# A two-image residual block: one statistics buffer shifted by 64 elements, two memsets dropped, one vector group moved behind another

## The chip, the cores and the metric

The kernel runs on one core of a Trainium2 chip. Its time is the device time of one execution in microseconds (us). Five engines work side by side, each through its own instructions in a fixed order, and wait for one another through semaphores: TensorE (PE in the profile: matmuls; PEld: its weight loads), VectorE (DVE), ScalarE (ACT), GpSimd (POOL) and SyncE (SP), which here only issues DMA transfers.

## The reference

Two images of 512 channels and 64x64 pixels go through a residual block of a diffusion network:

```
h   = conv3(silu(group_norm(x, g1, be1)), w1)        # 4 groups, 3x3 filters, zero padding
h   = h + (silu(t_emb) @ w_emb)[:, :, None, None]
out = x + conv3(silu(group_norm(h, g2, be2)), w2)
```

A group norm needs the mean and the variance of 128 channels x 4096 pixels before its first SiLU can start. Everything is bf16 at the edges.

## The kernel before

**Tiling.** The 512 channels are four tiles (`ct` 0 to 3) of 128 partitions. An image is worked in two chunks of 32 rows, so that there are eight chunks: first layer image 0 (chunks 0 and 1) and image 1 (2 and 3), then the second layer likewise. Nearly all data lies in one SBUF array, `ar`, at offsets that are worked out by hand; `Z` is a scratch region in it.

**Convolution.** It is a fast convolution in the row direction. From the rows of an input tile the vector engine makes transformed planes; TensorE multiplies each with transformed filters; results are combined again. For chunk 0 and tile `ct` the steps on DVE are eight instructions on a scratch buffer `WB[ct % 3]`:

- `k0ct`: one scaling of 2210 elements a partition (`rows_a`, line 678; issued by `ts`, L349);
- `row0ct`: three adds of 1040 elements (`rows_a`; `tt`, L345). The third gives planes 4 and 5;
- `rob0ct`: an add, a scaling of 520 elements, and two adds (`rows_b`, line 692). These give planes 0 to 3.

Tile 1's scratch is `WB[1]`, at `Z` to `Z + 2210`; tile 2's begins at `Z + 6528`.

**Opening.** ACT applies the SiLU to tile 0 and tile 1 (`silu00`, `silu01`), each followed by a small POOL memset of the padding column (`z00`, `z01`), for which `k00` and `k01` wait. The statistics of tiles 2 and 3 (`st02`, `st03`, in `stats0`, line 1131) go around the engines: ones- and Gram-matmuls on PE, an ACT Square over 2080 elements, a small DVE product with the identity (L1190), an ACT Identity over 260 elements of PSUM, a tiny fp32 matmul on PE, then small DVE and POOL steps (L466 to L491), and the SiLU of the tile. PE then runs 24 groups of three matmuls called `o` (planes 4 and 5 with three sets of filters, tile 0 first), and after that `u00` (planes 0 to 3, tile after tile). PE fills its wait ahead of them with dummy matmuls on `ones_bf`. Meanwhile DVE also transforms the filters (`w1_0`, `w1_1`: adds of 1536 elements).

**The second image's statistics.** `stats1` (line 1225) loads each tile of image 1 in two halves into `ZST` and `ZST + 2080`, and ACT reads each half twice (2080 elements, L368). The first of these loads is called `st10`; in the SP queue it stands behind five loads of filter pieces (`ld_ur..`) and ahead of more of them, of `a10` (the input of chunk 1, into `AB[0]`), of `w1_1` and of the following statistics loads.

**Order.** No scheduler runs. Each operation is recorded in a plan with a number, and `ORDER` (line 168), a string with two characters for each operation, gives the order in which all of them are issued; an engine takes its own from it. Waits are set by overlap of the memory that operations read and write: an operation waits for earlier ones in that order that touch the same elements.

Of the kernel before, what the change touches and what calls it, by code (L numbers as in the profile page):

```python
# [165 lines left out]


ORDER = (
    "0P0M000N2i0R0Q0O0n010S020304050607080m0T1I0l1F0c0k1G0i0r0d0j1H0o0q0p0e0s1K1J1L0t0u0f0v1M0w1N0V1O2b1P0x0y260W0z0-2Y0g0h1Q"
# [3 lines left out]
    "483F3j5g3H493k4m3G4A4g3Y5Y4o4B4n4C3X3l4D4f3I4E4p4F3J3_3M4q4I3s403K4J3L6d3m4K3o4r4L3r4M5a4i4y4_4N3N4O5b5h5i4P3u3O55454s41"
    "56424v4R575Z4t584h3v59515A4G6V524Q5B4H5C4w4-6r5F5j5G4u6e6f5H5l436s5I445J5c6t5K5m5L8C5M6X5n5k5u50465p4z5v8D5w4S6W5x8E5z5o"
    "5-4T4W535_BU4UBV60543P4V615d4X6263475r4Y5q645N6Y9H5O675E6g685D5s69BW5P3Q6A5t6C6i6D5Q5T5e6E6h5R6j6F5SBY6G6B6kBk9I6H5y7-6l"
    "6a6I5U6J6u4Z6m5V6Z6v6n6w939J6x6qBX6p6z666-6_BcBZBm7071Ba657273AM746K79Bl6oBd6L7A6bBb5f6cAN4a7BAO5W7CBR7E6M7F7D7G7H6N6Q7I"
    "7J7KBoBe7L7P6OBSBg6P7QDT6y6R7RDbBn7iBfBq7S6S757j76Bp7T7kBTDc7M7UBr7l785X7mBi7VBh7W7nBj7o7p8F7q7N7r7s8G7tDU7X7u778H7v7Y7w"
    "7ODe8I7xDd7y7Z8KDV8L8M7zDf7_808N8ODX8PF18QDh8RDj8W7a8XDg7b818Y7cDQ7d8Z838S8b828a8c8d8e9495848f8g8hDRA88i858m7e8n8T878o6T"
    "7f8J868pDl8U8q8k888u8rDSDW968s8jDZ8t979K8vDY989LA9AADkDa899M999N8VBD9P8A6U9Q9R9S9T9A9U8l9VDi9W9b8B7h8w9cF29B9dDn9e9CF99g"
    "8x9h9i9j9F8z9k9l9m8y9n9G9r8-9D9sF38_9O9t9X9uDmF5909YAB9vFHF49a7g9wBEBFDp9xDoAC9yADAP9pFA9EAQ9fAE9oAR9ZDC9zAFAS9q9-AUAHAV"  # L180
    "ATAW91AX9_AYAZAGAaA3AbAgA0AcAdAhAIA2AiF7FBBGAjA1F6AlFCAmBIF8DDDEAnAoAKApAqArAsAwA4FIAxDqAJAtA5AyBJAuAzBH92A-BKEmALA_AeBM"
    "B0B2BLB1AfBsB3BNA6BtFJAvDFBuBQB4BvBPBxByB8BzB5B-AkB_C0DHB7C1C2C6DGB6C7C8C4C9B9C3CEBwCFCADIBAC5CGFLCBA7CHE-GjBOCJCKCnFDCL"
    "CMCoE_CNGbCODJFKCPCqF0CQCICTCrDLCUCVCRCWFFCZCXFECaCSDKFGBCCbFNCsDMCcGKFMDrCCGlDsDNGdGkFOCdDtCpCDEnEoCtDPDuGcDODwDxDyDzCY"
    "D-D_E2E0E1GfEpE5CuCeE6E7CvGYE8EDGnE3CwCfEEI6GeCxGrGZEFChCyEqGmEGCiCgCzErEIGLGMEJEKC-GaELEMC_EsENEOEPCjESHuETEUEAEVE9EYGh"
    "E4CkD0EZDvEtBBGpEQEaGgEHEuEbGsI8EvFPGtD1GoERFQGiD2EWEwFRECGNFSD3EBGqFUD4EzFVFWGvFXFYEcEXFZIEFaFbFdFfHvHwIAFgFhFiEdIMFnEx"
    "I7FoD5GPGuFpEeFkFqEyEgFsEhFtEfFuGQFvFeFwFxFTGwFyFzEiFcG0G1IGG2G3I9G6GRFjEjD6GxG7F-GOIFFrG8GyFlF_G9IIG4ClGSGzCmD7ICG-D8IB"
    "G_GTH0IOFmINIUGAGVH2H3JXH4IHGXH5H6GUHBH7HAH8H9G5HxHDJYJZHEIDHFHGIJHLGBEkHMIKHIHCHNGCHHDAHOHzIVGEILGFHQGWHRHSElHTHUD9H-HV"
    "HWHXGDHaH_HbGGHcHdIPHgHPHyGHHhH1HKKqKrHiIWKpI0HeHjDBI1IXIcHZHJHkIdI2NrHYIeI5JaJbI4IfNqIhHfIiIjIkIlIYImInHlIoIsIrItIQIuHp"
    "IvHmI-IqIRIpI_HoHnIaJ0IxISIwJ1IgIZITI3J3JcJ4HqJ5J6GIJ7J8J9JAIyHrJDJCJEJeJFIbJ2JGJJIzJBJfJKJHJdJLJgJIKsKtJMJiJuJnJhJvJwJj"
    "JNJlJxKuJzJ-J_JOK0K1K2JPGJK3K4K8KwK9M5KAKBJkKGKvJRKHKxPTJQKIJSJmKJM6M7K5NONPPUJTKyKLKMK6KNK7KONNK-KPKQJyKRKzKSKDKVKWKKJo"  # L190
    "KXKYKCL2KbKTK_KcKUL1KZKdM8M9KeL0LAL3JpLBKEKfLCJUMALDKFJqLFLGLHKaLILJLELKLLMCLMLOLQNQNRJrLRHsLSLTKgLYMDLZMBMELaKhKkLbPBLN"
    "JsLdKjNmNlLeMGLfKiLgLhMFQiLiLPLjJtLkHtLnLoPCPDMHNoLpLqLtMJLuPRLULVKlLvNSQhLwMKMSLXMTLcNULlMUNTLmMVNVLxMXLWQPMYLrMZL4MaNW"
    "MbMcLsMdJWMeJVMiMjL5MkMlLyMqMINpMgMrMhLzMsM0KmL-MtNXMfKnMvL_MwL6MxMyMWMzNYM-MnM_QQQRMLMmN0M1N3KoN4N5N6N9NbNAMuMpNBN1NZNC"
    "N2MoNsN7NcNtNDPSL7PEPFNuN8NdNvOmNaNxNyNENzN-PGN_M2O0O1O2OnL8O4NFO5NIOpPHO6NGPIRuNHNkO7L9M4O9OANJQfOBOCODOEOFPJM3OGNwOKOL"
    "NKOMPKONOOMMO3OPQgOQORPLNMOTOqMNOUOVOWPMOXOYOZMOOaPVO8OrOoMPOHPWOsPQPXOSOIPYOJObPaPNPbPcQSQTPdOcOtPePfPgOuPhMQPjOdQUPkMR"
    "PlRsOePmNeOfRdRePoRcQVPpOhPqPrNfOgPsPtPZPuPPPvNLPzPiP-P_Q0QWQ1PwQ2Q3RtOiQ4Q6PnQ7Q8Q9QXQAOjQBQCT6PxQDQYQjPyOkQEQkPOUJQ5Ql"
    "NnNgQmQaRfRgQoQFSpQpOlQqQrQsQtQZQuQvQxQGNhQyQKQHQzQcQIQ-QbQJR0T4R1QwR2QeR3R4QdR5RhR6R7RBSqSrRCUIRDNiRERFRGQLRHQnRIRKQ_Rv"
    "RLRMRjQNRJRNRORPRiRQRRR8QMRkRwT5NjRxRlR9RSRyRmRzWjSsStRnR_QOS0RAS1S2S3RoT3S4S5S6RrSuS8RpS9U1U2RqSAUGSBSwSDSESvSFWiSGSxSH"
    "SISJRTSKSySOSPS7VEVFSQUHSRS-SSSTR-SURUSVSXU0SYSzRYSZSaSbRVScSdSeT1RXVDT7RWT8SCS_T9SLXwRZTATCT2SWRaTDTEOvTFOwTGSfOxSMTHTI"
    "TJOySNTLOzTMSgTKTNO-ShTORbO_SiSlTQVUTRTSP0TTSjP1TUP2TVP3SkTWP4T0TXTbVVTYTcP5TdP6TeP7P9TfP8TBTgPASmThU3U4TiTkVTTlTmTnTaSn"  # L200
    "ToTpTqTZTrUKTjULTsUMU5UNTtUPUQURTuUSUTTPUUU7UVSoUWUYUXU8UZU6U9UaTvWQVGVHUbUAUBUdUeVWUfTyUgUCUhTwUiUjUDTxWRWSUkUoUpVIUEUq"
    "UrUsUtUuUFUvWgUxUyUOTzUzU-UlU_V0WhV1VKV2T-VXUwVJVYV3VLVZUnXdVMVaUmUcVcVOWTWUVdVeVfVNVgVhT_ViV4XeXfVjVlVmVPVnV5XtWVVSVoV6"
    "VqVrVsVRVtV7YrWWYsVuVvVkVwVxV9V_WXW0VyW1W2W3W4V8W5WYW6W8VpW9VAYqWAWZWBWCVbWDWEVQVBWFW7WkaQV-WlWGWaWmWbXgXhWnVzXvWpWcWqWr"
    "WsWHWtWuXiWvWwWyWeWzWIYtYuW-a5Xja6bgXkW_WJXuX1X2X3WxX4X5WdZ7X6VCX7X8WLWMXCXlXDWKXEaPXFWfX9XGXHXIWNa4XJXLXmXMXNWoXOXoWOXP"
    "X0XQZ9XRXnXKXSXxXAXyXTXpXzXrYvX-ZAXsY0Y1Y2XBY3a7a8Y4Y5YxY6Y7Y9XUYAY8YwYBaNXVWPYCYyYEZ8YFXqYGYHYIYzYJXWbLbMYKbKYLY_YPXXYQ"
    "YRY-XYYSYTYUYMXZYVZ0YWYYYZZ1X_YaYba9YcXad0YdYeYfZBZ2XbZCYDaOZDYgYOZEaAYXZGcbccaBZHZIZJYNZKZLZ3ZMZNZPZOYhZQaCZRYiZScaaDYm"
    "ZUYjZVZWaFZXYlZYeGZZaEYkZaZbZfZcbdYnZgZhZiZjbNbOZkZlaHYoZmZoZpZdZqZrXcaGZsZtZuZFZeZvZnaRZ5aSaIZwfYaTZTYpZxaUbPbfaWaXaLaY"
    "aZaaZyabaccdcebeadbRafaJagbSahaVbQaia0bTZzakcualambUZ_anaoapbVZ-aqaraeaMavfXawbWaxayasazbYa-a_b0ajb2ctb3a1b4cfb5b6b7b8b9"
    "bZa2bhaub1bichbjbAcgbkcibmatbnbobpcjbqbXbrbsbtbBa3bvbwclbxe8bCbyckbGb-bDb_c0eHc1coc2bFc3c4bEc5c9bucAZ4e9cBbHcCcDcEc6cFcG"
    "bbcIbIcJcHc_cKcncLcMcNcpcOcPd1cQZ6d2d3cyd4c8d5bld6d7bcd8dAc7dBbJdCcvdDdEcRdFdGdHdLdIdMaKdNdOcSdPd9dQdRc-dSczbzcTdUdVdWcm"  # L210
    "cVdXdYdZcwcUdacxdbcWcsdedfcrdgcqdhdibadjcXdkdldqdrdsdtdKdTcYdudvdwdJfPdxdceIeDeJeKeFeLdmeMeAeNeEdzeOePfQeCeRdneBeSeTdddy"
    "eUeVeWeQcZeXeYdpecedd_eZeeefdoegehe0eiejeld-e2emeneoe1e3epeqe4eresevewexeye6ekezebe-e_f0eteaf5f6f7fRf8f2fUf9fAe5f1fBggeu"
# [1176 lines left out]
```

## Time and profile before

| | |
|---|---|
| median of 3 runs | 470.1 us (469.33 to 470.42) |
| profiled execution | 470.15 us |
| its span (first to last instruction) | 468.1 us |
| busy: PE, DVE, ACT, POOL | 447.1, 439.3, 407.4, 63.1 us |
| busy share: PE, DVE, ACT | 96%, 94%, 87% |
| granted TensorE clock, mean | 0.982 |
| DMA | 93.82 MB, 200 GB/s mean |

In the views that follow, times are us from the start of the span. A row of the timeline has start, length, engine, line, operation, what it writes and reads with shapes, how many instructions were merged (x), and in brackets how long the engine was idle just before and what released it. A row of the windows has the window, its length, then busy time and number of instructions of PE, PEld, DVE, ACT and POOL, the granted TensorE clock as a share of full speed, the DMA engines' busy share and GB/s. "SPq" is SyncE's queue issuing a transfer.

### The profile page before, as it was taken

To read this page: it belongs to the slowest core of one execution; us is meant where nothing else is said; L and a number is where in the kernel's file an instruction comes from. 1 tells how busy PE (TensorE), PEld (TensorE's weight loads), DVE (VectorE), ACT (ScalarE), POOL (GpSimd) and SP (SyncE) were. 2 spreads that over 40 slices of the span, in tenths; PEclk is the share of its full clock that TensorE was granted. 3 is DMA by queue.
4 is the path that set the end of the run, shared out by engine and by line. 5 is a ranking of instruction groups with operands and counts; after the bars stand their busy time and mean duration, and the time that the engine had idled before them with its cause. 6 is when DMAs were issued, how large, how long until landed. Compare 5 with 4: busy or idle time off the path is not lost. (4 is left out here: it accounts for less than half of the span.)

```text
span 468.1 us, 8191 instructions
## 1 busy us (share of the span) xinstructions
PE 447.1 (96%) x2904; PEld 284.9 (61%) x2904; DVE 439.3 (94%) x811; ACT 407.4 (87%) x611; POOL 63.1 (13%) x96
## 2 busy tenths in 40 slices
...
GB/s 325 249 239 153 114 143 221 71 181 244 152 242 192 195 149 138 181 310 158 297 220 212 298 316 106 230 261 235 157 267 164 252 268 223 195 182 110 143 135 91
DMA packets 45480, 93.82 MB, mean 200 GB/s; under 512 B 8704, under 2 KB 20352, under 8 KB 45440
## 3 DMA queue, kind: packets, MB, share of 16 engines
...
q8 instruction: 22, 0.36, 0.3%
q14 instruction: 18, 0.15, 0.1%
...
## 5 line engine op out<-in xcount | busy, mean ns | idle before, releaser
L398 PE MATMUL psum<-ar 128*128 128x256 f16 (+2 forms) x2771 | 424.6, 315 | 7.3 <-ACT ar L368 4.6
L345 DVE TENSOR_TENSOR ar<-ar 128x1024 f16<-128x1024 f16 (+7 forms) x630 | 411.5, 713 | 10.1 <-ACT ar L368 6.4
L398 PEld LDWEIGHTS <-ar 128*128 128x128 f16 (+1 forms) x2763 | 269.4, 98 | 159.1 <-issue 16.1
L368 ACT ACTIVATE ar<-ar 128x512 f16<-128x512 f16 (+6 forms) x186 | 189.4, 1059 | 23.2 <-DVE ar L345 21.8
L368 ACT ACTIVATE ar<-psum 128x512 f16<-128x512 f32 (+3 forms) x250 | 160.0, 695 | 24.1 <-PE psum L398 8.8
L368 ACT ACTIVATE ar<-ar,fs 128x2304 f16<-128x2304 bf16 (+1 forms) x32 | 74.3, 2324 | 4.4 <-DVE fs L491 4.1
L383 POOL DMA_DIRECT2D ar<-ar x26 | 30.2, 1184 | 116.1 <-DVE ar L345 94.0
L387 POOL MEMSET ar<- 128x65 f16 (+4 forms) x43 | 10.8, 262 | 207.9 <-ACT ar L368 199.4
L383 POOL DMA_DIRECT2D out_dram<-ar x15 | 18.7, 1244 | 47.3 <-DMA ar<-ar 31.8
L368 ACT ACTIVATION_READ_ACCUMULATOR ar<-psum 128x1 f32 x104 | 24.9, 239 | 0.0
L349 DVE TENSOR_SCALAR ar<-ar 128x520 f16<-128x520 f16 (+3 forms) x50 | 19.9, 407 | 3.9 <-POOL ar L387 3.9
L398 PEld LDWEIGHTS <-ones_bf 128*128 128x128 bf16 x88 | 9.4, 113 | 7.1 <-issue 1.9
L398 PE MATMUL psum<-fs,ones_neg 128*128 128x1 f32 (+3 forms) x36 | 5.7, 275 | 7.1 <-ACT ar L368 5.6
L398 PEld LDWEIGHTS psum<-fs,ones_neg 128*128 128x128 f32 x36 | 5.8, 236 | 8.5 <-ACT ar L368 6.7
L398 PE MATMUL psum<-ones_bf 128*128 128x512 bf16 x32 | 8.7, 436 | 1.1 <-DVE ones_bf L402 1.1
L398 PE MATMUL psum<-ar,ones_bf 128*128 128x260 bf16 x56 | 8.7, 313 | 0.0
L368 ACT ACTIVATION_READ_ACCUMULATOR ar<-ar 128x1 f32 x36 | 7.5, 209 | 0.0
L435 DVE CAST fs<-gparm 128x16 f32<-128x16 bf16 x1 | 3.1, 3104 | 2.8 <-DMA gparm<-in_params_dram 2.8
L476 POOL TENSOR_TENSOR fs<-fs 128x1 f32<-128x1 f32 x4 | 2.9, 735 | 20.1 <-DVE fs L474 19.9
L1121 DVE BATCH_NORM_STATS2 fs<-ar 128x6 f32<-128x512 bf16 x4 | 2.5, 682 | 1.0 <-DMA ar<-in_x_dram 1.0
L436 ACT ACTIVATE s_sb<-tparm 128x18 bf16<-128x18 bf16 x1 | 0.2, 218 | 3.0 <-DMA tparm<-in_t_emb_dram 3.0
L398 PE MATMUL psum<-ar,s_sb 128*2 128x512 bf16 x9 | 2.7, 377 | 0.0
(54 smaller groups left out, 24.5 us busy)
## 6 DMA issues: line engine op xcount, KB each, us to landing
...
```

The lines of the kernel that those rows point to most:

```text
L345: pl.op("DVE", 0.075 + 0.000521 * out.n, lambda: nc.vector.tensor_tensor(out=out.ap, in0=a.ap, in1=b.ap, op=op), regs(a, b), regs(out), name)
L349: pl.op("DVE", cost or 0.075 + 0.00026 * out.n, lambda: nc.vector.tensor_scalar(out=out.ap, in0=a.ap, scalar1=s, scalar2=None, op0=ALU.mul ...
L368: lambda: nc.scalar.activation(out=out.ap, in_=a.ap, func=func, scale=sc, **kw), regs(*rr), regs(*ww), name)
L383: lambda: eng.dma_start(out=out, in_=in_, **kw), regs(*r), regs(*w), name, lat=3.2 if sw else None, after=after, sw=sw, seq=seq)
L387: pl.op("POOL" if eng == "gpsimd" else "DVE", 0.08 + 0.0005 * out.n, lambda: e.memset(out.ap, v), (), regs(out), name)
L398: nc.tensor.matmul(out.ap, lhsT=lhsT.ap, rhs=rhs.ap, start=st, stop=sp, skip_group_check=True)
L435: nc.vector.tensor_copy(out=fs[:, GB:GB + 4 * CT], in_=gparm[:])
L436: nc.scalar.activation(out=s_sb[:], in_=tparm[:], func=ACT.Silu)
L476: pl.op("POOL", 0.85, lambda: nc.gpsimd.tensor_tensor(out=F(rs, n).ap, in0=N.ap, in1=F(NEGH, n).ap, op=ALU.pow), regs(N), regs(F(rs, n)), ...
L1121: pl.op("DVE", 0.61, lambda: nc.vector.bn_stats(out=q.ap, in_=e.ap), regs(e), regs(q), nm)
```

## The change

There are four edits.

1. `ZST`, the statistics buffer of the second image, begins at `Z + 2240` in place of `Z + 2176`. It occupied `Z + 2176` to `Z + 6336` and so shared 34 elements with tile 1's scratch (`Z` to `Z + 2210`); it now occupies `Z + 2240` to `Z + 6400`.
2. The staging buffer of `emb` moves from `Z + 6336` to `Z + 6400`, behind it.
3. Two POOL memsets of 2340 elements each, over the input buffers `AB[0]` and `AB[1]`, are dropped.
4. `ORDER` is written anew: all numbers shift by two because of the dropped memsets, and the eight DVE instructions of tile 1 in chunk 0 stand later. On PE, ACT, POOL and SP, and in the GpSimd DMA queue, the order of what is left is the same.

```diff
 ORDER = (
-    "0P0M000N2i0R0Q0O0n010S020304050607080m0T1I0l1F0c0k1G0i0r0d0j1H0o0q0p0e0s1K1J1L0t0u0f0v1M0w1N0V1O2b1P0x0y260W0z0-2Y0g0h1Q"
...
+    "0N002g0P0O0M0l010Q020304050607080k0R1G0j1D0a0i1E0g0p0b0h1F0m0o0n0c0q1I1H1J0r0s0d0t1K0u1L0T1M2Z1N0v0w240U0x0y2W0e0f1O130V"
...
-    ZST = Z + 2176
+    ZST = Z + 2240
...
-                d = A(Z + 6336, [[1, n * 512]], BF16)
+                d = A(Z + 6400, [[1, n * 512]], BF16)
...
-                mm([(pe, R(s_sb[:, i0 + i, :], K("s_sb"), 2), A(Z + 6336 + i * 512, [[1, 512]], BF16),
+                mm([(pe, R(s_sb[:, i0 + i, :], K("s_sb"), 2), A(Z + 6400 + i * 512, [[1, 512]], BF16),
...
     XB1 = [UREG[3] + ct * YF for ct in range(CT)]
-    for i in range(2):
-        memz("gpsimd", A(AB[i], [[1, AF]]), "az")
```

Read out of `ORDER`, the DVE instructions from the end of the statistics of tile 1 on, where "before" has the moved ones in capitals (`+` is the small last step of a chain, `stt` the L1190 product, `cp` the L466 copy):

```
before: K01 ROW01 ROW01 ROW01 ROB01 ROB01 ROB01 ROB01 w1_0 k00 w1_0 row00 st02.stt row00 w1_0 row00 st02.cp
        st02 st03.stt st02 rob00 st03.cp st02 st03 st02+ st03 rob00 w1_0 rob00 st03 k02 st03+ row02 row02 rob00
        row02 w1_1 k03 rob02 row03 row03 rob02 row03 rob03 w1_1 rob03 rob02 w1_0 rob02 rob03 w1_1 rob03 w1_2 k10
after:  w1_0 k00 w1_0 row00 st02.stt row00 K01 w1_0 row00 st02.cp ROW01 st02 st03.stt st02 rob00 ROW01 st03.cp
        st02 st03 st02+ st03 ROW01 rob00 w1_0 rob00 st03 k02 st03+ row02 row02 rob00 row02 w1_1 k03 rob02 row03
        row03 rob02 row03 ROB01 rob03 w1_1 ROB01 rob03 rob02 w1_0 ROB01 rob02 ROB01 rob03 w1_1 rob03 w1_2 k10
```

What each operation waits for changes in four places only: `st10` no longer waits for tile 1's row steps; the first load of the second layer's filters (`w2_00`, into the same region) waits for them in its place; `a10` and `a11`, the loads into `AB[0]` and `AB[1]`, no longer wait for the memsets.

More of the change, by code (lines that the diff above doesn't have):

```diff
@@ L168 @@
 ORDER = (
-    "0P0M000N2i0R0Q0O0n010S020304050607080m0T1I0l1F0c0k1G0i0r0d0j1H0o0q0p0e0s1K1J1L0t0u0f0v1M0w1N0V1O2b1P0x0y260W0z0-2Y0g0h1Q"
-    "150X1a1k1R1S1T1U1W1V1X1g1h1i1j3R0Z1l0_1m180U23111n3Z1o2D102E1d0Y1p2r090A0B0C0D0E0F2G0G0H0I0J0K0L1q122F1r131s2H2I1t4x1B1u"
-    "3T2J142j2K1v2L1w162M2N1x1y3U171C0b191E1A2O3S1Y1z2P1Z1-1b1_2Q2R4b1D1c201e2u1f4j3W212S22292U243a3b2T252A272V282t2e2W2x2X3V"
-    "2Z2f2C2a0a2c2l2d2m2B2-2n2_3w2k2o2g302q4e2w2s312h323q2p333n4d343c353d3x2v4c363y3e373f384k4l2z393A3g2y3B3h3E3C3i3p3z3t3D3-"
@@ L173 @@
[L173 to L212, printed above, removed]
@@ L213 @@
-    "fCe7fZfDfafbfEfcghfdf4fefSfffgfWfifhf3fjfkfVflhafTfmfnfGfofpftfFfqfufvfHfwfxfyfKfzfJfIf-g0g1fLg2g3g4g5g6g7fNf_gAfMgBgCfr"
-    "fOgDg8gEfsgFgGgHgMg9gJgNgOgIgPgQgRgSgKgTgXgigVgjgkgYgUglgmgngbgogagZgpgLgrgqgsgcgtgugvgwgxgWgyh0gzh1gdh2h3geh4h5g-gfh6h7"
-    "h9g_h8hAhBhChDhEhFhGhJhHhKhIhLhMhThOhUhPhXhWhVhQhZhRhYhShbhNhchdhghehhhf"
+    "0N002g0P0O0M0l010Q020304050607080k0R1G0j1D0a0i1E0g0p0b0h1F0m0o0n0c0q1I1H1J0r0s0d0t1K0u1L0T1M2Z1N0v0w240U0x0y2W0e0f1O130V"
+    "1Y1i3P1P0X1Q1R1j0z1k160S210_1l3X1m2B0-1S2C1b0W1n2p090A0B0C0D0E0F2E0G0H0I0J0K0L1o102D1p1T111q2F2G1r4v191s3R2H1U122h2I1t2J"
@@ new lines @@
+    "1u142K1V2L1v1w3S151A0Z171C182M3Q1W1x2N1X1y1Z1z2O2P4Z1B1a1-1c2s1d4h3U1_2Q20272S223Y3Z2R2328252T261e2r2c2U2v2V3T2X1f2d2A2Y"
+    "0Y2a2j2b1g2k292y2l1h2z3u2i2m2e2-2o4c2u2q2_2f303o2n313l4b323a333b3v2t4a343w3c353d364i4j2x37383e2w393f3C3A3g3n3x3r3B3y463D"
+    "3h5e3F473i4k3E484e3W5W4m494l4A3V3j4B4d3G4C4n4D3H3z3K4o4G3q3-3I4H3J6b3k4I3m4p4J3p4K5Y4g4w4z4L3L4M5Z5f5g4N3s3M53434q3_5440"
+    "4t4P555X4r564f3t574_584E6T504O594F5A4u4y6p5D5h5E4s6c6d5F5j416q5G425H5a6r5I5k5J8A5K6V5l5i5s4-445n4x5t8B5u4Q6U5v8C5x5m5y4R"
@@ new lines @@
+    "4U515zBS4SBT5-523N4T5_5b4V6061455p4W5o625L6W9F5M655C6e665B5q67BU5N3O685r6A6g6B5O5R5c6C6f5P6h6D5QBW6E696iBi9G6F5w7y6j6Y6G"
+    "5S6H6s4X6k5T6X6t6l6u919H6v6oBV6n6x646y6zBaBXBk6-6_BY637071AK726I77Bj6mBb6J786ZBZ5d6aAL4Y79AM5U7ABP7C6K7D7B7E7F6L6O7G7H7I"
+    "BmBc7J7N6MBQBe6N7ODR6w6P7PDZBl7gBdBo7Q6Q737h74Bn7R7iBRDa7K7SBp7j765V7kBg7TBf7U7lBh7m7n8D7o7L7p7q8E7rDS7V7s758F7t7W7u7MDc"
+    "8G7vDb7w7X8IDT8J8K7xDd7z7-8L8MDV8NE_8ODf8PDh8U7Y8VDe7Z7_8W7aDO7b8X818Q8Z808Y8a8b8c9293828d8e8fDPA68g838k7c8l8R858m6R7d8H"
@@ new lines @@
+    "848nDj8S8o8i868s8pDQDU948q8hDX8r959I8tDW969JA7A8DiDY879K979L8TBB9N886S9O9P9Q9R989S8j9TDg9U9Z897f8u9aF0999bDl9c9AF79e8v9f"
+    "9g9h9D8x9i9j9k8w9l9E9p8y9B9qF18z9M9r9V9sDkF38-9WA99tFFF29Y7e9uBCBDDn9vDmAA9wABAN9nF89CAO9dAC9mAP9XDA9xADAQ9o9yASAFATARAU"
+    "8_AV9zAWAXAEAYA1AZAe9-AaAbAfAGA0AgF5F9BEAh9_F4AjFAAkBGF6DBDCAlAmAIAnAoApAqAuA2FGAvDoAHArA3AwBHAsAxBF90AyBIEkAJAzAcBKA-B0"
+    "BJA_AdBqB1BLA4BrFHAtDDBsBOB2BtBNBvBwB6BxB3ByAiBzB-DFB5B_C0C4DEB4C5C6C2C7B7C1CCBuCDC8DGB8C3CEFJC9A5CFEyGhBMCHCIClFBCJCKCm"
@@ new lines @@
+    "EzCLGZCMDHFICNCoE-COCGCRCpDJCSCTCPCUFDCXCVFCCYCQDIFEBACZFLCqDKCaGIFKDpCAGjDqDLGbGiFMCbDrCnCBElEmCrDNDsGaDMDuDvDwDxCWDyDz"
+    "E0D-D_GdEnE3CsCcE4E5CtGWE6EBGlE1CuCdECI4GcCvGpGXEDCfCwEoGkEECgCeCxEpEGGJGKEHEICyGYEJEKCzEqELEMENChEQHsERESE8ETE7EWGfE2Ci"
+    "C-EXDtErB9GnEOEYGeEFEsEZGqI6EtFNGrC_GmEPFOGgD0EUEuFPEAGLFQD1E9GoFSD2ExFTFUGtFVFWEaEVFXICFYFZFbFdHtHuI8FeFfFgEbIKFlEvI5Fm"
+    "D3GNGsFnEcFiFoEwEeFqEfFrEdFsGOFtFcFuFvFRGuFwFxEgFaF-F_IEG0G1I7G4GPFhEhD4GvG5FyGMIDFpG6GwFjFzG7IGG2CjGQGxCkD5IAGyD6I9GzGR"
@@ new lines @@
+    "G-IMFkILISG8GTH0H1JVH2IFGVH3H4GSH9H5H8H6H7G3HvHBJWJXHCIBHDHEIHHJG9EiHKIIHGHAHLGAHFD8HMHxITGCIJGDHOGUHPHQEjHRHSD7HyHTHUHV"
+    "GBHYHzHZGEHaHbINHeHNHwGFHfG_HIKoKpHgIUKnH-HcHhD9H_IVIaHXHHHiIbI0NpHWIcI3JYJZI2IdNoIfHdIgIhIiIjIWIkIlHjImIqIpIrIOIsHnItHk"
+    "IyIoIPInIzHmHlIYI-IvIQIuI_IeIXIRI1J1JaJ2HoJ3J4GGJ5J6J7J8IwHpJBJAJCJcJDIZJ0JEJHIxJ9JdJIJFJbJJJeJGKqKrJKJgJsJlJfJtJuJhJLJj"
+    "JvKsJxJyJzJMJ-J_K0JNGHK1K2K6KuK7M3K8K9JiKEKtJPKFKvPRJOKGJQJkKHM4M5K3NMNNPSJRKwKJKKK4KLK5KMNLKyKNKOJwKPKxKQKBKTKUKIJmKVKW"
@@ new lines @@
+    "KAL0KZKRKzKaKSK_KXKbM6M7KcK-L8L1JnL9KCKdLAJSM8LBKDJoLDLELFKYLGLHLCLILJMALKLMLONONPJpLPHqLQLRKeLWMBLXM9MCLYKfKiLZP9LLJqLb"
+    "KhNkNjLcMELdKgLeLfMDQgLgLNLhJrLiHrLlLmPAPBMFNmLnLoLrMHLsPPLSLTKjLtNQQfLuMIMQLVMRLaNSLjMSNRLkMTNTLvMVLUQNMWLpMXL2MYNUMZMa"
+    "LqMbJUMcJTMgMhL3MiMjLwMoMGNnMeMpMfLxMqL-KkLyMrNVMdKlMtLzMuL4MvMwMUMxNWMyMlMzQOQPMJMkM-L_N1KmN2N3N4N7NZN8MsMnN9M_NXNAN0Mm"
+    "NqN5NaNrNBPQL5PCPDNsN6NbNtOkNYNvNwNCNxNyPENzM0N-N_O0OlL6O2NDO3NGOnPFO4NEPGRsNFNiO5L7M2O7O8NHQdO9OAOBOCODPHM1OENuOIOJNIOK"
@@ new lines @@
+    "PIOLOMMKO1ONQeOOOPPJNKOROoMLOSOTOUPKOVOWOXMMOYPTO6OpOmMNOFPUOqPOPVOQOGPWOHOZPYPLPZPaQQQRPbOaOrPcPdPeOsPfMOPhObQSPiMPPjRq"
+    "OcPkNcOdRbRcPmRaQTPnOfPoPpNdOePqPrPXPsPNPtNJPxPgPyPzP-QUP_PuQ0Q1RrOgQ2Q4PlQ5Q6Q7QVQ8OhQ9QAT4PvQBQWQhPwOiQCQiPMUHQ3QjNlNe"
+    "QkQYRdReQmQDSnQnOjQoQpQqQrQXQsQtQvQENfQwQIQFQxQaQGQyQZQHQ-T2Q_QuR0QcR1R2QbR3RfR4R5R9SoSpRAUGRBNgRCRDREQJRFQlRGRIQzRtRJRK"
+    "RhQLRHRLRMRNRgRORPR6QKRiRuT3NhRvRjR7RQRwRkRxWhSqSrRlRzQMR-R8R_S0S1RmT1S2S3S4RpSsS6RnS7T_U0RoS8UES9SuSBSCStSDWgSESvSFSGSH"
@@ new lines @@
+    "RRSISwSMSNS5VCVDSOUFSPSySQSRRySSRSSTSVT-SWSxRWSXSYSZRTSaSbScS_RVVBT5RUT6SASzT7SJXuRXT8TAT0SURYTBTCOtTDOuTESdOvSKTFTGTHOw"
+    "SLTJOxTKSeTITLOySfTMRZOzSgSjTOVSTPTQO-TRShO_TSP0TTP1SiTUP2S-TVTZVTTWTaP3TbP4TcP5P7TdP6T9TeP8SkTfU1U2TgTiVRTjTkTlTYSlTmTn"
+    "ToTXTpUIThUJTqUKU3ULTrUNUOUPTsUQURTNUSU5UTSmUUUWUVU6UXU4U7UYTtWOVEVFUZU8U9UbUcVUUdTwUeUAUfTuUgUhUBTvWPWQUiUmUnVGUCUoUpUq"
+    "UrUsUDUtWeUvUwUMTxUxUyUjUzU-WfU_VIV0TyVVUuVHVWV1VJVXUlXbVKVYUkUaVaVMWRWSVbVcVdVLVeVfTzVgV2XcXdVhVjVkVNVlV3XrWTVQVmV4VoVp"
@@ new lines @@
+    "VqVPVrV5YpWUYqVsVtViVuVvV7VzWVV-VwV_W0W1W2V6W3WWW4W6VnW7V8YoW8WXW9WAVZWBWCVOV9WDW5WiaOVyWjWEWYWkWZXeXfWlVxXtWnWaWoWpWqWF"
+    "WrWsXgWtWuWwWcWxWGYrYsWya3Xha4beXiWzWHXsW_X0X1WvX2X3WbZ5X4VAX5X6WJWKXAXjXBWIXCaNXDWdX7XEXFXGWLa2XHXJXkXKXLWmXMXmWMXNW-XO"
+    "Z7XPXlXIXQXvX8XwXRXnXxXpYtXyZ8XqX-X_Y0X9Y1a5a6Y2Y3YvY4Y5Y7XSY8Y6YuY9aLXTWNYAYwYCZ6YDXoYEYFYGYxYHXUbJbKYIbIYJYzYNXVYOYPYy"
+    "XWYQYRYSYKXXYTY-YUYWYXY_XzYYYZa7YaXYc-YbYcYdZ9Z0XZZAYBaMZBYeYMZCa8YVZEcZcaa9ZFZGZHYLZIZJZ1ZKZLZNZMYfZOaAZPYgZQcYaBYkZSYh"
@@ new lines @@
+    "ZTZUaDZVYjZWeEZXaCYiZYZZZdZabbYlZeZfZgZhbLbMZiZjaFYmZkZmZnZbZoZpXaaEZqZrZsZDZcZtZlaPZ3aQaGZufWaRZRYnZvaSbNbdaUaVaJaWaXaY"
+    "ZwaZaacbccbcabbPadaHaebQafaTbOagZ-bRZxaicsajakbSZzalamanbTZyaoapacaKatfVaubUavawaqaxbWayaza-ahb0crb1Z_b2cdb3b4b5b6b7bXa0"
+    "bfasa_bgcfbhb8cebicgbkarblbmbnchbobVbpbqbrb9a1btbucjbve6bAbwcibEbybBbzb-eFb_cmc0bDc1c2bCc3c7bsc8Z2e7c9bFcAcBcCc4cDcEbZcG"
+    "bGcHcFczcIclcJcKcLcncMcNc_cOZ4d0d1cwd2c6d3bjd4d5bad6d8c5d9bHdActdBdCcPdDdEdFdJdGdKaIdLdMcQdNd7dOdPcydQcxbxcRdSdTdUckcTdV"
```

5 lines of the change are left out of this document (added).

## The prediction

> **What bounds the kernel now.** I read the busy shares first (PE 96%, DVE 94%, ACT 87%: three engines near full), then the windows, to see where each is not.
>
> ```profile
> 23.00:28.00 5.00, 0.00 (x0) 0.00 (x0) 4.93 (x11) 0.00 (x0) 0.00 (x0) 1.00 0.36 122
> 28.00:34.00 6.00, 5.43 (x24) 4.10 (x25) 3.39 (x9) 4.26 (x7) 0.99 (x2) 0.50 0.90 291
> 34.00:40.00 6.00, 6.00 (x20) 2.30 (x21) 4.95 (x14) 5.72 (x6) 0.72 (x2) 0.65 0.44 181
> 40.00:60.00 20.00, 20.00 (x93) 8.77 (x92) 19.80 (x31) 19.73 (x25) 0.46 (x3) 1.00 0.40 130
> 60.00:100.00 40.00, 40.00 (x186) 17.53 (x185) 36.85 (x68) 39.71 (x57) 3.09 (x5) 1.00 0.47 144
> 100.00:140.00 40.00, 39.86 (x235) 22.83 (x233) 38.71 (x88) 38.15 (x72) 4.12 (x6) 1.00 0.74 219
> 140.00:300.00 160.00, 155.22 (x1000) 97.62 (x999) 158.71 (x292) 156.71 (x290) 12.48 (x25) 1.00 0.68 215
> ```
>
> From 23 to 28 us PE and ACT do nothing and DVE everything; then PE runs at half clock. From 35 on ACT and PE are full, from 100 on DVE too. An opening that ends earlier can thus move all that follows. The timelines of ACT, PE and SP's queue say what the hole waits for:
>
> ```profile
> 19.42 1.92 ACT L368 ACTIVATE ar<-ar 128x2080 fp8e4<-128x2080 bf16 x1
> 28.04 0.39 ACT L368 ACTIVATE ar<-psum 128x260 bf16<-128x260 f32 x1 [6.61 <-DVE ar L1190]
> 28.41 1.93 ACT L368 ACTIVATE ar<-ar 128x2080 fp8e4<-128x2080 bf16 x1
> 32.14 0.39 ACT L368 ACTIVATE ar<-psum 128x260 bf16<-128x260 f32 x1 [1.71 <-DVE ar L1190]
> ```
> ```profile
> 19.95 2.98 PE L398 MATMUL psum<-ones_bf 128*128 128x512 bf16 x13
> 28.57 1.44 PE L398 MATMUL psum<-fs,ones_neg 128*128 128x2 f32 x6 [5.64 <-ACT ar L368]
> 31.56 1.49 PE L398 MATMUL psum<-ar 128*128 128x512 f16 x3
> ```
> ```profile
> 25.17 0.33 SPq L383 DMA_DIRECT2D ar<-in_x_dram  x1
> ```
>
> ACT's Identity of st02 waits 6.61 us for DVE's L1190 product; PE, out of fill matmuls at 22.93, waits 5.64 for that Identity; the first `o` matmul starts at 31.56. And DVE:
>
> ```profile
> 16.69 0.21 DVE L491 SCALAR_TENSOR_TENSOR fs<-fs 128x1 f32<-128x1 f32 x1
> 19.78 0.74 DVE L349 TENSOR_SCALAR ar<-ar 128x2210 f16<-128x2210 f16 x1 [2.87 <-POOL ar L387]
> 20.55 2.91 DVE L345 TENSOR_TENSOR ar<-ar 128x1040 f16<-128x1040 f16 x4
> 23.50 0.30 DVE L349 TENSOR_SCALAR ar<-ar 128x520 f16<-128x520 f16 x1
> 23.83 2.18 DVE L345 TENSOR_TENSOR ar<-ar 128x1040 f16<-128x1040 f16 x3
> 27.65 0.29 DVE L1190 SCALAR_TENSOR_TENSOR ar<-psum,ident 128x128 bf16<-128x128 f32 x1
> ```
>
> It idles 2.87 us for tile 1's SiLU and padding memset, works tile 1's eight instructions to 25.14 (these release `st10` at 25.17, which had blocked SP since 13.47), and reaches the product only at 27.65.
>
> **The change, part by part.** Spacings are start to start in this trace: an add of 1040 elements 0.61 us (0.73 behind the one it needs), of 1536 elements 0.87, `k` 0.64, the 1536 scaling 0.47, the 520 scaling 0.21, chain steps 0.08 to 0.15.
>
> *DVE's new order.* Its next slot is 16.83. Tile 0's SiLU ends at 17.31 and its memset by 17.5, so: filter add 16.83, `k00` 17.70, scaling 18.34, `row00` 18.81, product 19.42 (16.83 + 0.87 + 0.64 + 0.47 + 0.61). The filter data are there: PE multiplies a tile loaded behind them at 13.42. ACT's Square ends at 21.35, after the product (19.71): the Identity moves from 28.04 to 21.35, by 6.69, and its wait is gone.
>
> *What is late next.* PE's fills end first: the tiny matmuls run from 22.77 (six at 0.11, as at 12.09 where 12 took 1.47 with their drain) to 23.57. DVE, done with the third `row00` at 22.44, idles to 23.68 for the copy, then works one `row01`. PE's eight ones-matmuls for st03 end at 24.5, DVE's second product runs 24.54 to 24.83, the second Identity starts at 24.88 (now 32.14). It has waited 1.04 in place of 1.71: 7.26 earlier. The Square of `st10` follows at 25.25. DVE's last step of st02 ends by 27.0, before that Square (27.17), so `silu02` follows without its present 0.28 wait: 27.17 for 34.81, which is 7.64 earlier. From here ACT has no wait on DVE until 139.4; two waits on PE, 0.21 at 51.15 and 0.23 at 60.20, go if PE gains more than ACT: 7.64 + 0.23 = 7.87, or 8.08 with the 0.21 too. I count the 0.23 alone: the operation at 51.15 also needs DVE's last `rob02` add but one, which comes at 42.8 for a slot at 43.3.
>
> *PE.* First `o` at about 24.3, no hole of 5.64, full clock. Tile 2's `o` need `row02` at 33.2 (PE there at 33.3), tile 3's `row03` at 37.47 (0.3 wait). Their start moves from 47.07 to 37.5, by 9.5: PE leads, ACT follows.
>
> *DVE behind that.* To `row03` it follows ACT's SiLUs, 7.64 earlier (45.11 becomes 37.47). Then come tile 1's last four instructions, at 0.61 + 0.21 + 0.61 + 0.61 = 2.04: `k10` comes at 46.3 for 51.88, only 5.6 earlier. Tile 1's last add ends at 43.4; PE wants it at 44.1. DVE then has waits to eat up:
>
> ```profile
> 64.07 1.91 DVE L345 TENSOR_TENSOR ar<-ar 128x1024 f16<-128x1024 f16 x3 [0.58 <-ACT ar L368]
> 81.82 0.68 DVE L1103 COPY ar<-psum 2x512 f32<-2x512 f32 x1 [2.06 <-PE psum L398]
> ```
>
> Both end when ACT and PE are done, which now lead DVE by over 2 us: 5.6 + 0.58 + 2.06 = 8.2, level with ACT by 82 us. Bounds: if nothing is caught up the gain is 5.6; it cannot pass ACT's 8.1 while ACT is full (39.71 of 40.00 between 60 and 100). I take ACT's 7.87: the two waits together, 2.64, are longer than the 2.3 that DVE lacks.
>
> *Transfers.* Without the overlap `st10` waits only for SP's turn (13.47) and for the slot of an earlier x load, which PE uses by 16.29 at the latest; 4.7 us to landing (that group's median) gives 21.0 for a use at 25.25. The filter pieces and `a10` behind it come 9 to 11 us earlier too, into a window with DMA busy 0.35. `ld_ur3` still waits for PE's st03 matmuls (24.5); the second half of `st10`, next to it, has 8.6 us until ACT wants it, against 8.95 now. `emb`'s first load still waits for tile 2's `rob02`, now 42.7: with 2.6 to landing 45.3, for PE at 46.7. The wait passed on to `w2_00` costs nothing: SP issues no `w2` load before 90.06, and tile 1 is done at 43.4.
>
> *The memsets.* POOL spends 4.08 us on them and a third, small one from 3.77. DVE's L435 cast takes 3.10 us and ends at 7.88, just as they do; without them DVE would be free some 3 us sooner, but its next work waits for x until 8.85 anyway: gain 0. Loss: `a10` and `a11` never waited for them in practice. Bounds: 0, and the 0.96 that DVE waits for x, should x land sooner without them; I take 0, since that wait is a transfer's. The Trainium skill, page "SBUF — State Buffer", says that the pair of ports DVE shares with GpSimd is locked exclusively for a whole instruction; the cast's 3.10 us agrees, and by that rule too the sum stays.
>
> *Does it reach the end?* After 100 us the waits alternate between DVE, ACT and PE (DVE 0.48 at 112, ACT 1.71 at 139, PE 0.97 at 163) and transfers are issued by their progress, so a shift of all three stays. **Sum:** 470.15 - 7.87 = 462.28, **462.3 us**. The profiled execution stands 0.05 above the median of 470.1, which I neglect.
>
> **Rivals.**
> - *DVE does not catch up* (its waits at 64 and 82 turn out to belong to chains through DVE itself): 470.15 - 5.6 = 464.6. For: DVE is full after 100. Against: both waits name ACT or PE.
> - *PE's clock falls anyway.* The clock was halved from 14.3 to 17.7 us, after an idle of only 1.42 and twelve tiny matmuls; the new opening has six tiny ones at 22.8, a 0.4 wait at 25.2 and six more. At half clock from 24.6 to 34.8 PE does 18 `o` matmuls at 0.43 where 35 would fit; all 72 end at 45.9, 5.05 earlier than now (50.95), and ACT's evacuation at 60.20 gains the like, 5.2: 465.0. The Trainium skill, "TensorE: Matmul & The Clock Gate", Part 1, asks for an idle window of about 3.4 us before the clock halves; by that rule there is no fall here and the sum stands. The row after 1.42 speaks against it as the only condition.
> - *The buffer is not really free* (slower). If `st10` still waited for tile 1's scratch, its release would be 43.4 and not 25.14, and SP, in order, would hold it and all behind it. ACT's Square of it stands ahead of `silu02`: 43.4 + 4.7 = 48.1 against 32.51, so +15.6: 485.7. It costs from a landing at 25.25 on, that is a release at 20.5, and eats the whole gain at a release of 28.4. Against: tile 1 ends at Z + 2210, the buffer begins at Z + 2240 and ends at Z + 6400, short of tile 2's scratch at Z + 6528.
> - *PE is the bound, not ACT*: its 9.5 carried through would give 460.7. Against: ACT's 39.7 of 40.
>
> **How the numbers follow.** Mine 0.60; DVE not caught up, or half of it, 0.17; half clock 0.10; PE-bound 0.03; a delay that leaves no gain within 0.2% 0.04 (something in DVE's queue between 24 and 44 that I place wrongly by 7 us); slower 0.06 (the buffer, or the same delay at 10 us). The range 461.5 to 465.2 holds mine and the first two rivals, 0.87 less what falls just outside. Faster by over 0.2%: 0.60 + 0.17 + 0.10 + 0.03 = 0.90; same 0.04; slower 0.06. 0.2% (0.9 us) is about what a measurement of this kernel can tell: its runs span 469.33 to 470.42.
>
> **What would show it.** Right: ACT's Identity of st02 near 21.4 without a wait; PE's hole of 5.64 gone, first `o` near 24.3 and the clock at 1.00 between 28 and 38; `st10` issued before 17; `silu02` near 27.2; DVE's 2.06 wait at L1103 gone; a span near 460.2. Wrong: PE waiting on DVE around 44 (`rob01`), SP's queue standing still until 43, ACT waiting for DVE between 27 and 139, or a shift of 8 us at 60 that shrinks later: then DVE's own work, and not the opening, sets the end.

## The result and the profile after

| | before | after |
|---|---|---|
| median (6 runs each, same chip) | 469.72 us (468.92 to 470.43) | 461.81 us (460.75 to 463.17) |
| ratio after/before, 95% interval | | 0.9834 (0.9811 to 0.9858) |
| profiled execution | 470.15 us | 460.75 us |
| its span | 468.1 us | 458.8 us |
| busy: PE, DVE, ACT | 447.1, 439.3, 407.4 us | 442.3, 435.3, 407.0 us |
| granted TensorE clock, mean | 0.982 | 0.997 |

The medians differ by 7.91 us; 7.87 had been forecast. The windows of the kernel after, for the first stretches (columns as before):

```profile
23.00:28.00 5.00, 4.75 (x29) 2.61 (x27) 4.78 (x17) 4.75 (x7) 1.93 (x3) 1.00 0.87 306
28.00:34.00 6.00, 6.00 (x30) 2.73 (x28) 5.63 (x11) 6.00 (x5) 0.35 (x2) 1.00 0.52 176
34.00:40.00 6.00, 5.76 (x28) 2.53 (x27) 5.97 (x12) 6.00 (x6) 0.18 (x1) 1.00 0.17 66
60.00:100.00 40.00, 39.19 (x192) 18.34 (x191) 39.29 (x74) 39.94 (x59) 4.12 (x5) 1.00 0.58 170
```

From 23 to 28 us, where PE and ACT had done nothing, both are busy for 4.75 of 5.00, at full clock. Between 60 and 100 us DVE has gone from 36.85 to 39.29 of 40: its spare time there is used up, and PE (40.00 to 39.19) now gives way a little. The timelines of ACT, of PE and of SP's queue in the kernel after:

```profile
21.43 0.36 ACT L368 ACTIVATE ar<-psum 128x260 bf16<-128x260 f32 x1
24.06 0.39 ACT L368 ACTIVATE ar<-psum 128x260 bf16<-128x260 f32 x1 [0.25 <-DVE ar L1188]
26.36 2.29 ACT L368 ACTIVATE ar<-ar,fs 128x2304 f16<-128x2304 bf16 x1
```
```profile
18.55 2.98 PE L398 MATMUL psum<-ones_bf 128*128 128x512 bf16 x13
21.94 0.83 PE L398 MATMUL psum<-fs,ones_neg 128*128 128x2 f32 x6 [0.42 <-ACT ar L368]
23.53 0.81 PE L398 MATMUL psum<-ar 128*128 128x512 f16 x3
```
```profile
14.51 0.33 SPq L383 DMA_DIRECT2D ar<-in_x_dram  x1
```

ACT's Identity of `st02` comes at 21.43 without a wait (28.04 after 6.61 before), `silu02` at 26.36 (34.81), PE's first `o` at 23.53 (31.56), and `st10` is issued at 14.51 (25.17). The product is L1188 here, since two lines are gone.

One thing differs that the edit did not make: the fill matmuls end at 21.53 here and at 22.93 in the profile of before, because that execution had a half-clock stretch from 14.3 to 17.7 us and this one had not. The kernel after was therefore profiled a second time, together with some of the experiments, and that execution (463.06 us, span 461.3) has the stretch too. One of its windows, then the timelines of PE, of ACT, and of DVE at L1103:

```profile
14.40:17.80 3.40, 3.40 (x26) 2.76 (x25) 3.35 (x10) 2.69 (x2) 1.05 (x5) 0.50 1.03 396
```
```profile
20.07 2.98 PE L398 MATMUL psum<-ones_bf 128*128 128x512 bf16 x13
22.88 0.72 PE L398 MATMUL psum<-fs,ones_neg 128*128 128x2 f32 x6
24.37 0.81 PE L398 MATMUL psum<-ar 128*128 128x512 f16 x3
37.53 2.75 PE L398 MATMUL psum<-ar 128*128 128x512 f16 x12 [0.24 <-DVE ar L345]
```
```profile
21.44 0.37 ACT L368 ACTIVATE ar<-psum 128x260 bf16<-128x260 f32 x1
24.90 0.39 ACT L368 ACTIVATE ar<-psum 128x260 bf16<-128x260 f32 x1 [1.08 <-DVE ar L1188]
27.20 2.29 ACT L368 ACTIVATE ar<-ar,fs 128x2304 f16<-128x2304 bf16 x1
```
```profile
73.24 0.67 DVE L1103 COPY ar<-psum 2x512 f32<-2x512 f32 x1
```

This is the execution to set beside that of before. How much earlier the same operation starts in it, ACT's operations in order:

| operation (start before) | forecast | measured |
|---|---|---|
| Identity of `st02` (28.04) | 6.69 | 6.60 |
| Identity of `st03` (32.14) | 7.26 | 7.24 |
| `silu02` (34.81) | 7.64 | 7.62 |
| behind the 0.21 wait on PE (51.15) | 7.64 (7.85) | 7.95 |
| behind the 0.23 wait on PE (60.20) | 7.87 (8.08) | 8.28 |
| from 63 to 110 us | 7.87 | 8.43 |
| from 112 to 270 us | 7.87 | 7.86 to 7.91 |
| the end | 7.87 | 6.80 |

### The profile page after: what moved, and what is told of

The parts are those of the page before. It is cut to its first block, busy times and chain, and to the rows that moved or that the text cites. A ratio compares the mean times of both kernels' runs of the same rounds, so it can differ in the third digit from the quotient of the medians.

```text
span 458.8 us, 8186 instructions
## 1 busy us (share of the span) xinstructions
PE 442.3 (96%) x2904; PEld 281.7 (61%) x2904; DVE 435.3 (95%) x811; ACT 407.0 (89%) x611; POOL 59.6 (13%) x94
## 5 line engine op out<-in xcount | busy, mean ns | idle before, releaser
L387 POOL MEMSET ar<- 128x65 f16 (+3 forms) x41 | 6.8, 177 | 206.5 <-ACT ar L368 196.8
L398 PE MATMUL psum<-ar,ones_bf 128*128 128x260 bf16 x56 | 7.1, 274 | 0.0
L398 PEld LDWEIGHTS psum<-fs,ones_neg 128*128 128x128 f32 x36 | 4.6, 191 | 3.1 <-ACT ar L368 1.7
L398 PE MATMUL psum<-fs,ones_neg 128*128 128x1 f32 (+3 forms) x36 | 4.6, 246 | 1.7 <-DVE fs L1124 1.0
```

Of the source, the lines that this page charges most:

```text
L387: pl.op("POOL" if eng == "gpsimd" else "DVE", 0.08 + 0.0005 * out.n, lambda: e.memset(out.ap, v), (), regs(out), name)
L398: nc.tensor.matmul(out.ap, lhsT=lhsT.ap, rhs=rhs.ap, start=st, stop=sp, skip_group_check=True)
```

## Experiments

The kernel before measured 469.66 to 469.91 us in the jobs below; ratios are to it. The kernel after, once more:

> The changed kernel itself once more, on the same chip as its variants. Theory: 460.7 to 463.2, in two groups by what the clock record shows in the opening: those with a half-clock stretch near 14 us some 1.4 us longer than those without. Rival (the two groups have nothing to do with the clock): times and mean granted clocks that do not go together.

Measured: 461.75 us (460.32 to 463.06, 5 runs), ratio 0.9815 (0.9787 to 0.9843). Two of the five runs lie below the range that was expected. The stretch costs less than 1.4 us: with it everything to 102 us comes 0.84 later than without it (`silu02` 27.20 against 26.36). The fills start 1.52 later (20.07 against 18.55), but in the execution without the stretch PE waits 0.42 for ACT ahead of its six tiny matmuls, and this wait takes part of the delay up: they start 0.94 later (22.88 against 21.94), and what they release 0.84. That the times fall into two groups by this stretch is not shown: this execution also lost 0.55 to a transfer at 103 us and 1.05 to a second half-clock stretch at 270.4, and time and mean clock do not go together in every run (461.75 and 460.32 us both had 0.997).

**Part by part.** Four kernels take the change apart. The first drops the memsets from the kernel before, the second only moves the buffer:

```diff
-    for i in range(2):
-        memz("gpsimd", A(AB[i], [[1, AF]]), "az")
```

> The kernel before without the two POOL memsets, nothing else. Theory (the opening is set by DVE's order, the memsets are covered): no change, ratio to before 0.999 to 1.001, although DVE's L435 cast falls from 3.10 to about 0.2 us, because the next DVE work waits for x until 8.9 us; the ACT wait before the Identity of st02 stays at 6 to 7 us. Rival (the memsets cost something of their own, since the first matmuls and the clock of TensorE also differ between the two profiles before 17 us: no half-clock stretch at 14.3 after the change): 0.8 to 1.4 us faster, ratio 0.997 to 0.998.

Measured: 469.85 us, ratio 1.0002 (0.9986 to 1.0018). The cast L435 shrinks from 3.10 to 0.17 us, and ACT's 6.61 wait stays to the hundredth. The memsets are worth nothing here.

```diff
-    ZST = Z + 2176
+    ZST = Z + 2240
-                d = A(Z + 6336, [[1, n * 512]], BF16)
+                d = A(Z + 6400, [[1, n * 512]], BF16)
```

> The kernel before with the statistics buffer and the staging buffer 64 elements later, the order of before kept. Theory: SyncE no longer stands still from 13.5 to 25.2 us and the transfers behind st10 land 9 to 11 us earlier, but nothing was waiting for them: ratio 0.999 to 1.001, ACT's first wait still 6 to 7 us and its Square of st10 still near 32.5. Rival (the freed queue is what gains): at least 1.5 us faster, ratio below 0.997.

Measured: 470.52 us, ratio 1.0008 (0.9995 to 1.0022). `st10` is issued at 14.33 in place of 25.17, and nothing follows from it: ACT reads `st10` behind the second Identity, which still waits for DVE.

The next two put tile 0 ahead of tile 1 but keep tile 1's eight instructions together, without memsets; first with the old buffer, then with the new one. The DVE order from tile 1's statistics on, read out of `ORDER`:

```diff
-K01 ROW01 ROW01 ROW01 ROB01 ROB01 ROB01 ROB01 w1_0 k00 w1_0 row00 st02.stt row00 w1_0 row00 st02.cp st02 st03.stt ...
+w1_0 k00 w1_0 row00 st02.stt row00 K01 w1_0 row00 ROW01 ROW01 ROW01 ROB01 ROB01 ROB01 ROB01 st02.cp st02 st03.stt ...
```

> Tile 0 first on DVE, but all eight instructions of tile 1 follow in one piece after the third row00 and before the st02 copy, with the buffer where it was before the change; no memsets. (The order of after itself cannot be had with the old buffer: ACT reads st10 ahead of silu02, DVE does k02 ahead of the last rob01, and st10 would wait for that rob01.) Theory, from the rows of after: the second product of DVE slips from 23.7 to 27.25, st10 is released at about 27.1 and lands 3.3 us later (as at 25.17 to 28.43 before), so ACT's Square of st10 starts near 30.4 and silu02 near 32.3, 5.9 later than after and about 2.5 earlier than before: 467 to 468.5 us, ratio 0.993 to 0.998. Rival (the order is all, the buffer nothing): the same time as e4.

> The DVE order of e3 with the buffer of after, so that the two differ in the buffer alone. Theory: silu02 near 29.9, 3.5 later than after; ACT then sets the shift, and DVE, which has no rob01 left over, is about level with it: 464.5 to 466 us, ratio 0.988 to 0.992, about 2.4 us faster than e3. Rival 1 (the buffer nothing): equal to e3. Rival 2 (what counts is only that PE's hole closes, since its matmuls then run at full clock): as after, ratio 0.983.

Measured: 467.97 us, ratio 0.9955 (0.9941 to 0.9968), with the old buffer; 465.11 us, ratio 0.9899 (0.9883 to 0.9916), with the new one. ACT in the kernel with the old buffer, and ACT and PE in that with the new one:

```profile
30.52 1.94 ACT L368 ACTIVATE ar<-ar 128x2080 fp8e4<-128x2080 bf16 x1 [6.41 <-DMA ar<-in_x_dram]
```
```profile
29.05 2.31 ACT L368 ACTIVATE ar<-ar,fs 128x2304 f16<-128x2304 bf16 x1 [3.03 <-DVE fs L491]
```
```profile
27.53 0.83 PE L398 MATMUL psum<-fs,ones_neg 128*128 128x2 f32 x6 [3.29 <-DVE ar L1188]
```

With tile 0 first the old buffer becomes the limit: tile 1 now ends later, so `st10` is issued at 26.96, and ACT stands 6.41 us for its landing. Of the two orders, only in this one is the shift worth something, 2.86 us. With the new buffer the wait moves on to DVE: the second product stands behind all of tile 1 and comes at 27.19, where the kernel after has it at 23.73. The three steps are 1.9 (order), 2.9 (buffer, given the order) and 3.3 us (tile 1 spread out behind the later chains, 465.11 to 461.8, the last from two jobs).

The change's own order could not be tried with the old buffer. `st10` would wait for tile 1's last step; that stands behind `k02` in DVE's order, `k02` needs `silu02`, and ACT has `silu02` behind the Square of `st10`: a circle.

**What sets the end.** One more Square on ACT, and three more scalings `k10` on DVE, each in both kernels:

```diff
                 act(junk(), d, ACT.Square, scale=float(HW) ** -0.5, acc=F(part + 2 + i), name=nm)
+                if ct == 0 and i == 1:
+                    act(junk(), d, ACT.Square, scale=float(HW) ** -0.5, acc=F(WARM + 1), name=nm)
```

> The changed kernel with one more Square of ACT (1.92 us) over the second half of st10, behind the one that is there; its sum goes to a column that nobody reads. Theory (ACT is full from the opening on and sets the end): plus 1.9 us, so 463.7. Rival (DVE, which after the changed order has only two waits of 0.4 and 0.5 us left before 110 us, sets the end): plus 0, since DVE does not wait for ACT between.

> The kernel before with the same extra Square of ACT (1.92 us). Theory (there too ACT sets the end, full from 35 us on but for waits of 0.21 and 0.23): plus 1.5 to 1.9 us, 471.4 to 471.8. Rival (DVE's line of work is as late as ACT's there, and has room of its own): plus 0 to 0.5.

Measured: after 463.29 us (kernel after 461.75 in that job), plus 1.54; before 471.60, ratio 1.0045 (1.0032 to 1.0058), plus 2.1 (1.5 to 2.7). In the first pair the runs overlap (460.32 to 463.06 and 462.55 to 464.86 us), so the traces are the better measure there. The second profile of the kernel after has the same half-clock stretch in its opening; DVE's row that waits for ACT at 83 us, there and with the added Square:

```profile
83.19 1.23 DVE L345 TENSOR_TENSOR ar<-ar 128x2048 f16<-128x2048 f16 x1 [0.42 <-ACT ar L368]
```
```profile
85.32 1.23 DVE L345 TENSOR_TENSOR ar<-ar 128x2048 f16<-128x2048 f16 x1 [1.15 <-ACT ar L368]
```

It moves by 2.13, which is the whole addition (the SiLU behind it on ACT goes from 35.43 to 37.55). At 115 us the difference is down to 1.70 (114.92 to 116.62), since the second profile of the kernel after had by then lost its 0.55 to the transfer at 103. ACT's line of work sets the end in both kernels.

```diff
-        scal(keng, A(w, [[1, KF]]), A(ab, [[1, KF]]), 4.0, f"k{c}{ct}")
+        for _ in range(4 if c == 1 and ct == 0 else 1):
+            scal(keng, A(w, [[1, KF]]), A(ab, [[1, KF]]), 4.0, f"k{c}{ct}")
```

> The changed kernel with tile 1's k10 scaling (0.64 us on DVE, at 45.3 us) done four times over, plus 1.9 us of DVE. Theory (the catching up has used the waits of 0.58 and 2.06 us that DVE had in the kernel before; what is left are 0.41 at 82 and 0.48 at 103 us): plus 1.0 to 1.8 us. Rival (DVE has as much room as before): plus 0 to 0.3.

> The kernel before with the k10 scaling done four times over (plus 1.9 us of DVE at 52 us). Theory (DVE's waits of 0.58 at 64 us and 2.06 at 82 us take it up): plus 0 to 0.3 us. Rival (DVE has no room there either, so that its catching up in the changed kernel came from something else): plus 1.0 to 1.9, as the same addition cost in the changed kernel (1.7).

Measured: after 463.48 us, plus 1.73; before 469.42 us, ratio 0.9996 (0.9982 to 1.0011), plus nothing. The addition was 2.33 us (one scaling takes 0.73, the four 3.05). DVE and ACT in the kernel after with the scalings, and DVE in the kernel before with them (L1104 is `emb`'s L1103, one line on):

```profile
45.18 3.05 DVE L349 TENSOR_SCALAR ar<-ar 128x2210 f16<-128x2210 f16 x4
```
```profile
53.22 1.48 ACT L368 ACTIVATE ar<-ar 128x1536 bf16<-128x1536 bf16 x1 [1.62 <-DVE ar L345]
```
```profile
64.67 2.50 DVE L345 TENSOR_TENSOR ar<-ar 128x1024 f16<-128x1024 f16 x4
80.85 0.67 DVE L1104 COPY ar<-psum 2x512 f32<-2x512 f32 x1
```

In the kernel before the waits of 0.58 and 2.06 swallow the addition whole: both are gone. (This execution had a faster opening than the profile of before, so its times are not to be compared row by row: ACT is 1.10 earlier at 59 us.) In the kernel after they had been spent on tile 1; a 0.41 wait at 82 us was left and goes, ACT stands 1.62 for DVE, and the rest is seen (in the traces ACT is 1.95 later from 61 us on). So in the kernel after DVE is level with ACT, and either costs nearly in full.

**The clock, and the rest.** The memsets put back into the kernel after:

> The changed kernel with POOL's two memsets put back. Theory (they are worth nothing, since x lands at 8.9 us in any case): the time of the changed kernel, 461 to 462.5. Rival (the free cast or the free early DMA is worth something in the new order, or the memsets disturb the clock's windows): plus 0.8 to 1.4 us.

Measured: 461.62 us, ratio 0.9834 (0.9821 to 0.9848): nothing, as in the kernel before. The cast takes 3.30 us again and DVE's first statistics step starts at 8.80 with a wait for x of 0.91, where it was 8.95 with 4.06.

Fewer fill matmuls in the kernel after (and `ORDER` without their numbers), 8 and then 17 of 21:

```diff
-    'fill': 21,
+    'fill': 8,
```

> The changed kernel without the 13 fill matmuls of 128x512 that keep PE busy from 18.5 to 21.5 us, so PE is idle there for some 3 us. Theory (ACT's line of work sets the end; PE comes to tile 3's `o` about 1.9 us ahead of what it needs, as its waits of 0.24 at 36.69 us and the copies behind it show): the clock falls to half for one or more stretches after about 22 us; each stretch of 3.4 us takes 1.7 us of PE's work, of which about 1.9 lie beside ACT, so the time is the changed kernel's plus 0 to 1.5 us, up to 3 if the half clock lasts 10.2 us as it did in the kernel before. Rival (PE is the bound): all that the clock takes is seen, plus 1.7 to 5 us. Rival (the early clock is worth nothing at all): plus 0 even with a half-clock stretch of 6 us or more in the trace.

> The changed kernel with four of its 21 fill matmuls left out, so that the fills end 0.9 us earlier: at 22.0 us in executions with a half-clock stretch near 14.4 us, at 20.6 in those without. Theory (in the first kind the fills' end, and not ACT, releases the six tiny matmuls at 22.8; PE's idle of 0.4 to 1.3 us in their place brings no further half clock): minus 0.7 to 0.9 us in the executions with the stretch, 0 in those without, so 461.0 to 461.7 in the median. Rival (the longer idle brings a half-clock stretch at 22 us, as 13 fills fewer did): plus 0.8 in those where it does.

Measured: 462.54 us with 8 (kernel after 461.75), 461.75 us with 17 (kernel after 461.75 and 461.81 elsewhere). PE and the windows in the profile with 17:

```profile
18.68 2.12 PE L398 MATMUL psum<-ones_bf 128*128 128x512 bf16 x9
22.08 0.83 PE L398 MATMUL psum<-fs,ones_neg 128*128 128x2 f32 x6 [1.28 <-ACT ar L368]
```
```profile
14.40:17.80 3.40, 3.40 (x41) 2.99 (x40) 3.35 (x9) 2.56 (x2) 1.10 (x5) 1.00 1.03 399
23.10:29.90 6.80, 6.80 (x24) 3.52 (x22) 5.44 (x18) 5.72 (x8) 2.04 (x4) 0.50 0.70 260
```

With 8 fills PE idles 3.33 us ahead of the tiny matmuls and the clock is halved from 22.5 to 25.9; the second Identity comes at 24.94, 0.88 late. The medians differ by 0.8 us, which is less than the runs of either kernel spread. With 17 fills an idle of 1.28 us was followed by half clock for 6.8 us in the execution profiled (463.66 us, the slowest of its five), while the fastest (460.30 at a mean clock of 0.997) had next to none. No gain in the median: the rival held in the one execution that shows it. The saving that was expected with a half-clock stretch near 14 us could not be seen, since the execution profiled has no such stretch. No version here beats the kernel after by more than its runs scatter.

## Why the prediction was right

*DVE's new order* held to a tenth. The product came at 19.51 (19.42 forecast) and the Identity at 21.43 (21.35).

*What is late next* held in the execution with the same opening: second product 24.57 (24.54), second Identity 24.90 (24.88), `silu02` 27.20 (27.17). Its step "PE's fills end first" silently took over the half-clock stretch of the profile of before, which the edit has nothing to do with. In the first profile of the kernel after, which has no such stretch, the fills end at 21.53, and `silu02` comes 0.84 earlier. The two waits on PE were under-sized: taken together 7.62 became 8.43, by 0.81, where 0.23 had been counted. The 0.21 that was left out did go, each of the two steps is 0.33, and a third of 0.15 follows at 62.77, where the wait was 0.03. Each is 0.10 to 0.12 more than the wait shown: an operation of ACT that does not wait starts before the one ahead has ended (in the kernel after at 21.79, where the one ahead runs from 21.70 to 21.89), and a wait costs this overlap too.

*PE* held: first `o` at 24.37 (24.3), tile 3's `o` at 37.53 (37.5) behind a wait of 0.24 (0.3).

*DVE behind that* held: from 50 us on it is 5.72 earlier (5.6 forecast for `k10`), and at L1103 8.58 (8.2 forecast), where both waits are gone (the lag behind ACT, 2.2 at 50 us, is made good by 73). That these waits are what it lived on is shown by the scalings: free in the kernel before, 1.73 us in the kernel after. The rival in which DVE does not catch up falls with it.

*Transfers* held: `st10` at 14.51 (16.3 at the latest) and no transfer late before 100 us. But the term was not as harmless as its sum of nothing: with the order alone the old buffer cost 2.86 us.

*The memsets* held, in both kernels. The cast takes 0.17 or 0.18 us alone and 3.10 to 3.37 beside the memsets. The Trainium skill, "SBUF — State Buffer", section "SBUF: two separate sides", says that the pair of ports DVE shares with GpSimd is an exclusive lock, held for a whole instruction while the other engine blocks. The cast agrees in that it was held up; but in the profile of before it began during the first of three memsets (4.78 us), which ended at 5.81, and it was not done before the third had ended (7.88 against 7.85).

*Does it reach the end?* The shift does carry on, yet not as the forecast had it. It is 7.87 at 112 us because 0.56 more had been gained and 0.55 was lost to a wait of 0.63 on a filter load at 103 us, which the first profile of after does not have; and 1.05 is lost at a half-clock stretch from 270.4 to 273.8, which neither first profile has. Against the first profile of the kernel after, which has neither loss nor the stretch in the opening, the span is 9.25 shorter. The forecast lies between the two executions, as the medians' 7.91 does; that it comes within 0.04 us is luck, with smaller terms that offset each other.

*The rivals.* Half clock between 24 and 38 us did not come in any of the five profiled executions with all 21 fills and this order (both of after, memsets back, ACT more, DVE more), where PE's idles are 0 to 0.42; behind 1.28 and 3.33 it did. The mechanism of this rival was real, then, and the new opening stayed on the safe side of it. The Trainium skill, "TensorE: Matmul & The Clock Gate", Part 1, asks for an idle window of about 3.4 us and has it run freely; the second half agrees with the stretches here, the first does not: 1.28 us of idle and six tiny matmuls were enough. The buffer rival was wrongly priced: had `st10` still waited for tile 1, the order would have been a circle and not 15.6 us slower. PE as the bound falls: the added Square on ACT cost 1.54, and PE then stood 2.19 us waiting for ACT at 43.76.
